# The hidden layer of an MLP by a seven-product form over pairs of chunks, with the output product three pairs behind and interleaved

## The chip, the cores and the metric

One NeuronCore of a Trainium2 chip runs the whole program. The metric is the device time of one launch in microseconds (us), from the first to the last instruction with what lies around it. Two versions count as different here when they differ by more than 0.2%.

## The reference, cut to what matters

Three layers follow one another on 4 x 3072 tokens of width 256: a Fourier mixing layer, a gated layer with hidden width 1024, and an MLP with hidden width 2048. Only the last one is touched:

```
n_tokens, d_model, d_ff = (1536, 256, 2048)     # sizes by which the weights are scaled
...
def _moe2_ref(x, w_in, w_out) -> np.ndarray:
    h = x @ w_in                                  # here x is 12288 x 256, w_in 256 x 2048
    sp = np.where(h > 20.0, h, np.log1p(np.exp(np.minimum(h, 20.0))))
    g = h * np.tanh(sp)                           # Mish
    return (g @ w_out).astype(np.float32)         # w_out 2048 x 256
```

## The kernel before, in words

Every float32 matmul operand is held as two parts, a rounded high part and the remainder (type fp32r), and a product is three matmuls: high by high, high by low, low by high. The table `P3` lists these three.

The MLP is the last stage. The 12288 tokens are cut into 24 tiles (`NBLK`) of 512 columns, and the 2048 hidden features into 16 chunks of 128. A *pair* `P` is two neighbouring chunks of one tile, so a tile has 8 pairs and the stage 192. The input of a tile, `x2`, is 128 partitions by 2 halves of d by 512 tokens; VectorE (DVE) splits it into `x2h` (`split_x2`, line 885). For each pair `emit_h` (line 890) runs `h_mm` twice (line 693 holds the matmul): 2 halves of d times 3 matmuls of 128 x 512 into one PSUM bank. `g_ev` then lets ScalarE (ACT) evaluate Mish twice from PSUM, once rounded into `gh` (line 713) and once in full into `g` (line 714), and DVE subtracts them to `gl` (line 715). `emit_o` (line 898) multiplies `gh` by both parts of `w_out` (one matmul of 512 columns, line 909) and `gl` by the high part (256 columns, line 910), eight such couples per pair, and adds into four PSUM banks `o0` to `o3` that are kept over the tile. At the last pair of a tile `o_out` empties them: an ACT copy (line 923), a DVE add (line 924) and a DMA, for each of the four.

The order is written out by hand: no scheduler moves an instruction, and each engine works through its own queue in the order in which the Python code emits it. The loop over pairs emits h of pair `P`, then the output product of pair `P - LAG`:

```
    LAG = 2
    for P in range(2, 8 * NBLK + LAG):
        ...
            emit_h(P)
            if q == 4 and t + 1 < NBLK:
                split_x2(t + 1)
        emit_o(P - LAG)
```

Pairs 0 and 1 are computed earlier, inside the end of the gated layer. The eight PSUM banks are four for `o` and four for h, which rotate (`bufs=4`).

Of the kernel before, what the change touches and what calls it, by code (L numbers as in the profile page):

```python
# [24 lines left out]
NBLK = B * 6  # L25
# [4 lines left out]
def kernel(  # L30
# [27 lines left out]
    nc = tc.nc  # L58
# [543 lines left out]
    for u in range(NU + 3):  # L602
# [25 lines left out]
        if u in S1_AT:  # L628
            i = 8 + S1_AT[u]
# [28 lines left out]
    def x2h_tile(t):  # L658
        pool = pb if t % 2 else w2p
        x2h_t[t] = pool.tile([128, 2, 2, 512], F32R, tag="x2h", name="x2h", bufs=1)  # L660
        return x2h_t[t]
# [14 lines left out]
    P3 = ((0, 0), (0, 1), (1, 0))  # L676
    g_t = {}
# [9 lines left out]
    def h_mm(f0, p):  # L687
# [3 lines left out]
        for dh in range(2):  # L691
            for (w, v) in P3:
# [3 lines left out]
                )  # L696
                i += 1

    def g_ev(P, ps):

        pool, n = (w2p, 2) if P % 5 < 2 else (pb, 3)
        gh = pool.tile([128, 2, 512], F32R, tag="gh", name="gh", bufs=n)
        gl = pool.tile([128, 2, 512], F32R, tag="gl", name="gl", bufs=n)
# [12 lines left out]
        g_t[P] = (gh, gl)  # L716
# [22 lines left out]
    def emit_k(P):  # L739
        t, i2 = divmod(P, 4)  # L740
        hl = xk_t[t]
        p = psap.tile([128, 2, 512], F32, tag="k", name="kp", bufs=2)
        for m in range(2):
            f = 2 * i2 + m
            i = 0
            for dh in range(2):
                for (w, v) in P3:
                    nc.tensor.matmul(  # L748
                        out=p[:, m, 0:TA], lhsT=WK[:, dh, w, f * 128:(f + 1) * 128], rhs=hl[:, v, dh, :],
                        start=(i == 0), stop=(i == 5),  # L750
                    )
                    i += 1
        kp_t[P] = p
# [43 lines left out]
    def pp():  # L797
        return psap.tile([128, 4, 256], F32, tag="p", name="pp")
# [3 lines left out]
    for t in range(NA + 1):  # L802
        live = t < NA
        nxt = t + 1 < NA
        new = (t + 2) % 8 == 0 and t + 2 < NA
        if new:
            load_Dp((t + 2) // 8)
        for i2 in range(4):
            P = 4 * t + i2
            if live:  # L810
                emit_k(P)
            if 0 <= P - 2 < 4 * NA:
                emit_v(P - 2)
            then = None

            if nxt:
                if i2 == 0:
                    if put:
                        put()
                        put = None  # L820
                    is2_ev(t + 1, 0)
                    is2(t + 1, 1, pp())
                elif i2 == 1:
                    if new:
                        split_Dp((t + 2) // 8)
                    is2_ev(t + 1, 1)
                    delta()
                    if t + 2 < NA:
                        split_D(t + 2)
                elif i2 == 2:  # L830
                    if t > 0:
                        v_ev(t - 1)
                    r_ev(t)
                    if new:
                        prefix((t + 2) // 8, pp()[:, 0:2, :])
                    if t + 2 < NA:
                        split_IF(t + 2)
                    then = shift(t + 1, "xk")
                else:
                    if new:  # L840
                        put = prefix_ev()
                    if t + 2 < NA:
                        is2(t + 2, 0, pp())
                    then = shift(t + 1, "xr")
            elif i2 == 2:
                v_ev(t - 1)
                if live:
                    r_ev(t)
            if i2 == 1 and live:
                emit_r(t)  # L850
            if t == NA - 2 and i2 == 2:
                bg(1 << 20)
                x20 = pap.tile([128, 2, 512], F32, tag="dec_raw", name="x20", bufs=1)
                nc.sync.dma_start(out=x20, in_=x2_part(0, 512))
            if t == NA - 1 and i2 == 0:
                hl = x2h_tile(0)
# [17 lines left out]
    pb = ctx.enter_context(tc.tile_pool(name="pb", bufs=1, side="left", reuse_waits="tile"))  # L874
    psb = ctx.enter_context(tc.tile_pool(name="psb", bufs=1, space=PSUM, reuse_waits="tile"))
    out_v = out.rearrange("(b m w j n) d -> b j m n w d", b=B, m=3, w=32, j=8)

    x2_t, o_t = {}, {}
# [6 lines left out]
    def split_x2(t):
        v = x2_t.pop(t)
        hl = x2h_tile(t)
        split(v, hl[:, 0], hl[:, 1], nc.vector, nc.vector)
# [32 lines left out]
    def o_out(t, m):  # L921
        o, ob = o_t[t][m], ob_t[t]
        nc.scalar.copy(out=ob[:, m, :], in_=o[:, 1, :])
        nc.vector.tensor_tensor(out=ob[:, m, :], in0=ob[:, m, :], in1=o[:, 0, :], op=ALU.add)
        nc.sync.dma_start(out=out_dst(t, m), in_=ob[:, m, :])

    ob_t = {}
    LAG = 2
    load_x2(1)
    load_x2(2)  # L930
    for P in range(2, 8 * NBLK + LAG):
        t, q = divmod(P, 8)
        if P < 8 * NBLK:
            if q == 0 and 2 < t + 2 < NBLK:
                load_x2(t + 2)
            emit_h(P)
            if q == 4 and t + 1 < NBLK:
                split_x2(t + 1)
        emit_o(P - LAG)
# [82 lines left out]
```

## Time and profile before

| what | value |
|---|---|
| median of 3 runs | 2101.23 us (2100.57 to 2104.56) |
| the profiled execution's own time | 2103.25 us |
| its span, first to last instruction | 2101.4 us |
| matmuls (PE) busy | 2051.0 us, 98% of the span |
| weight loads (PEld) busy, beside the matmuls | 1853.3 us, 88% |
| VectorE (DVE) busy | 1108.2 us, 53% |
| ScalarE (ACT) busy | 1069.1 us, 51% |
| GpSimd (POOL) busy | 29.6 us, 1% |

The MLP is roughly the second half of the span, from about 1025 us on. A share of busy time is an average over stages, so what the change is worth has to be read from that half. The recorded length of a matmul (for example 394 ns) covers its way through the array; the next one starts before it ends, so the time that a matmul costs is the distance from its start to the next start, its pitch. In rows that merge several instructions ("x12") the length runs to the start or end of the last.

### The profile page before, as it was taken

The page shows a single profiled execution, that of the slowest core. Times are in us where ns is not written, and L with a number is a line of the kernel's source. Part 1 is how long each engine was busy: PE and PEld are TensorE (multiplying, and loading weights), DVE is VectorE, ACT ScalarE, POOL GpSimd, SP SyncE. Part 2 cuts the span into 40 slices and gives each one's busy share as a digit, 9 for nine tenths or more (in the row PEclk, how much of TensorE's full clock was granted, in tenths as well). Part 3 has the DMA queues.
Part 4 walks back from the last instruction along what each step waited for, and adds up shares of the span by engine and source line. Part 5 has one row for each costly group of instructions (what it writes and reads, how often), then busy time and mean ns, then how long its engine had stood idle before and what let it go on. Part 6 is the DMA issues. An engine that isn't in the chain of part 4 may idle for free.

```text
span 2101.4 us, 28565 instructions
## 1 busy us (share of the span) xinstructions
PE 2051.0 (98%) x11628; PEld 1853.3 (88%) x11628; DVE 1108.2 (53%) x1601; ACT 1069.1 (51%) x1815; POOL 29.6 (1%) x48
## 2 busy tenths in 40 slices
PE   6999998999999999999999999999999999999998
PEld 5999998999999999999988888888888888888887
DVE  5899996787777877776422223222323223223222
ACT  5566655666666666666444434444444344443443
POOL 1000000000000000000000000000000000000000
PEclk6999999999999999999999999999999999999999
DMA  8567532112121121111100000000000000001000
GB/s 249 160 192 209 171 111 74 57 50 73 46 72 51 58 63 56 57 47 44 46 21 21 25 26 21 31 21 21 29 23 30 21 21 21 31 21 31 11 11 20
DMA packets 71476, 122.86 MB, mean 58 GB/s; under 512 B 6193, under 2 KB 48433, under 8 KB 71345
## 3 DMA queue, kind: packets, MB, share of 16 engines
q1 hardware_dynamic: 66864, 105.31, 16.9%
q0 software_dynamic: 4480, 15.73, 2.0%
q8 instruction: 91, 1.49, 0.3%
q14 instruction: 41, 0.33, 0.1%
HBM read 70.69 MB, written 50.33 MB: 58 GB/s over the span
## 4 chain that ended last, share of the span: by engine, by line
PE 79%; DVE 12%; ACT 4%; issue 2%; DMA 2%; SPq 0%; ACTq 0%; DVEq 0%; POOLq 0%
PE hp L693 25%; PE o L909 17%; PE o L910 9%; PE vp L786 8%; PE kp L748 7%; PE mxp L361 5%; PE s2p L315 2%; PE pp L725 2%; PE pp L466 1%; DVE kl L773 1%; PE s1p L274 1%; DVE kr L768 1%; ACT kh L76 1%; PE i1p L385 1%; DVE Dl L77 1%
## 5 line engine op out<-in xcount | busy, mean ns | idle before, releaser
L715 DVE TENSOR_TENSOR gl<-g,gh 128x1024 fp32r<-128x1024 f32 x190 | 232.8, 1225 | 755.1 <-ACT g L714 755.1
L693 PE MATMUL hp<-x2h,WI 128*128 128x512 f32 x2280 | 560.5, 394 | 0.0
L909 PE MATMUL o<-WO,gh 128*128 128x512 f32 x1536 | 546.8, 395 | 0.0
L713 ACT ACTIVATE gh<-hp 128x512 fp32r<-128x512 f32 x380 | 227.2, 598 | 601.8 <-PE hp L693 601.8
L693 PEld LDWEIGHTS hp<-x2h,WI 128*128 128x128 f32 x2280 | 415.2, 188 | 93.0
L910 PE MATMUL o<-WO,gl 128*128 128x256 f32 x1536 | 429.7, 280 | 0.0
L909 PEld LDWEIGHTS o<-WO,gh 128*128 128x128 f32 x1536 | 288.0, 188 | 68.7
L910 PEld LDWEIGHTS o<-WO,gl 128*128 128x128 f32 x1536 | 289.1, 188 | 8.5
L748 PE MATMUL kp<-xk,WK 128*128 128x384 f32 x1536 | 293.0, 339 | 0.0
L786 PE MATMUL vp<-kh,WV 128*128 128x384 f32 x1024 | 283.7, 338 | 6.1 <-DVE r L794 5.9
L748 PEld LDWEIGHTS kp<-xk,WK 128*128 128x128 f32 x1536 | 269.0, 190 | 0.1
L714 ACT ACTIVATE g<-hp 128x512 f32<-128x512 f32 x380 | 225.1, 592 | 0.0
L786 PEld LDWEIGHTS vp<-kh,WV 128*128 128x128 f32 x1024 | 186.3, 188 | 12.7 <-DVE r L794 12.6
L786 PE MATMUL vp<-kl,WV 128*128 128x384 f32 x512 | 171.6, 335 | 0.0
L361 PE MATMUL mxp<-WX,Xh 128*128 128x256 f32 x752 | 140.0, 286 | 0.0
L76 ACT CAST kh<-kr 128x768 fp32r<-128x768 f32 x64 | 53.5, 836 | 153.1 <-DVE kr L768 150.6
L761 ACT ACTIVATE kr<-kp 128x768 f32<-128x768 f32 x128 | 103.9, 812 | 38.5 <-PE kp L748 36.9
L361 PEld LDWEIGHTS mxp<-WX,Xh 128*128 128x128 f32 x752 | 118.5, 194 | 0.2
L361 PE MATMUL mxp<-WX,Xl 128*128 128x256 f32 x376 | 107.1, 285 | 0.0
L773 DVE TENSOR_TENSOR kl<-kr,kh 128x768 fp32r<-128x768 f32 x64 | 62.7, 980 | 69.1 <-ACT kr L772 69.1
L786 PEld LDWEIGHTS vp<-kl,WV 128*128 128x128 f32 x512 | 96.2, 188 | 0.0
L77 DVE TENSOR_TENSOR kl<-kr,kh 128x768 fp32r<-128x768 f32 x64 | 61.4, 959 | 61.4 <-ACT kh L76 61.4
(127 smaller groups left out, 2326.3 us busy)
## 6 DMA issues: line engine op xcount, KB each, us to landing
xs<-in_x_dram SPq DMA_DIRECT2D x32, 384.0 KB
A<-scr SPq DMA_DIRECT2D x48, 256.0 KB
scr<-Cs SPq DMA_DIRECT2D x48, 256.0 KB
D<-scr SPq DMA_DIRECT2D x32, 384.0 KB
x2d<-r POOLq DMA_DIRECT2D x32, 384.0 KB, 3.5
x<-x2d SPq DMA_DIRECT2D x24, 512.0 KB
out_dram<-ob SPq DMA_DIRECT2D x96, 128.0 KB
scr<-st SPq DMA_DIRECT2D x24, 384.0 KB
```

What stands on the lines that cost most here:

```text
L77: (lo_eng or nc.vector).tensor_tensor(out=lo, in0=src, in1=hi, op=ALU.subtract)
L361: nc.tensor.matmul(out=p[:, e, :], lhsT=a, rhs=WX[:, dh, c, w, :], start=(i == 0), stop=(i == 11))
L693: nc.tensor.matmul(out=p, lhsT=WI[:, dh, w, f * 128:(f + 1) * 128], rhs=hl[:, v, dh, :], start=(i == 0), stop=(i == 5),)
L713: nc.scalar.activation(out=gh[:, m, :], in_=p, func=AF.Mish)
L714: nc.scalar.activation(out=g[:, m, :], in_=p, func=AF.Mish)
L715: nc.vector.tensor_tensor(out=gl, in0=g, in1=gh, op=ALU.subtract)
L748: nc.tensor.matmul(out=p[:, m, 0:TA], lhsT=WK[:, dh, w, f * 128:(f + 1) * 128], rhs=hl[:, v, dh, :], start=(i == 0), stop=(i == 5),)
L761: nc.scalar.activation(out=kr, in_=v, func=AF.Relu)
L773: nc.vector.tensor_tensor(out=kl, in0=kr, in1=kh, op=ALU.subtract)
L786: nc.tensor.matmul(out=p[:, o, 0:TA], lhsT=WV[:, f, w, o * 128:(o + 1) * 128], rhs=v[:, m, :], start=(f == 0 and i == 0), stop=(f == 7 and ...
L909: nc.tensor.matmul(out=o[m], lhsT=gh[:, m2, ms], rhs=WO[:, f], start=(f == 0), stop=False)
L910: nc.tensor.matmul(out=o[m][:, 0, :], lhsT=gl[:, m2, ms], rhs=WO[:, f, 0, :], start=False, stop=(f == 15))
```

## The change

Tile 0 keeps the old form. From tile 1 on, a pair of chunks, the two halves of d and the two halves of the tile's 512 columns form 2 x 2 blocks on each side, and h is computed with seven block products in place of eight. A block product (`prod` in `emit_hS`) is three matmuls of 128 x 256, so a pair has 21 of them in place of 12 of 128 x 512. The sums of weight blocks (`WS`, four per pair, high and low part) are made once during tile 0 by `make_WS`; the sums of input blocks (`xS`, seven blocks, high and low part) are made for every tile by `make_xS` in six pieces during the tile before. The products fall into four PSUM banks: `p1` (bank h0), `pA` (h1), `pB` (h2) and `pC` (h3), each with one buffer. ACT copies `p1` to SBUF, and four DVE additions put the quarters together in the SBUF tile `C3`, from which Mish is now read (two activations of 128 x 1024 in place of four of 128 x 512). Mish and the subtraction of pair `P` are emitted inside pair `P + 1`. The output product is the same work, now three pairs behind and cut into eight steps, which stand between the products: 2, 3 and 3.

```
@@ g_ev: buffers @@
+    def g_tiles(P):
+        pool = w2p if P % 4 < 2 else pb
+        return [pool.tile([128, 2, 512], F32R, tag=n, name=n, bufs=2) for n in ("gh", "gl")]
-        pool, n = (w2p, 2) if P % 5 < 2 else (pb, 3)
...
-            g = pb.tile([128, 2, 512], F32, tag="g", name="g", bufs=3)
+            g = pb.tile([128, 2, 512], F32, tag="g", name="g", bufs=2)
@@ new functions; split_x2 and x2h_tile go @@
+    WS = pb.tile([128, 8, 4, 2, 128], F32R, name="WS")
+    def make_WS(q):
+        a = pb.tile([128, 2, 2, 2, 128], F32, tag="C3", name="wa", bufs=2)
+        w = WI[:, :, :, 512 * q:512 * (q + 1)]
+        fl = a.rearrange("p j r i n -> p j (r i n)")
+        nc.vector.tensor_tensor(out=fl, in0=w[:, :, 0, :], in1=w[:, :, 1, :], op=ALU.add)
+        sm = pb.tile([128, 2, 4, 128], F32, tag="C3", name="ws", bufs=2)
+        for k, x0, x1, op in (
...
+        ):
+            nc.vector.tensor_tensor(out=sm[:, :, k, :], in0=x0, in1=x1, op=op)
+        split(sm, WS[:, 2 * q:2 * q + 2, :, 0, :], WS[:, 2 * q:2 * q + 2, :, 1, :])
+    def make_xS(t, k):
...
+        if k == 0:
+            sub(0, b12, b11)
+            sub(2, b22, b12)
+        elif k == 1:
+            sub(1, b22, xT[:, 0, :])
+            sub(3, b21, xT[:, 1, :])
+        elif k == 2:
+            nc.vector.tensor_copy(out=xS[:, 0, 3:7, :], in_=xT)
+        elif k == 3:
+            nc.vector.tensor_tensor(out=xS[:, 1, 3:7, :], in0=xT, in1=xS[:, 0, 3:7, :], op=ALU.subtract)
+        elif k == 4:
+            nc.vector.tensor_copy(out=xS[:, 0, 0, :], in_=b11)
+            nc.vector.tensor_copy(out=xS[:, 0, 1:3, :], in_=b2)
+        else:
+            nc.vector.tensor_tensor(out=xS[:, 1, 0, :], in0=b11, in1=xS[:, 0, 0, :], op=ALU.subtract)
+            nc.vector.tensor_tensor(out=xS[:, 1, 1:3, :], in0=b2, in1=xS[:, 0, 1:3, :], op=ALU.subtract)
...
-            p = psb.tile([128, 512], F32, tag="h", name="hp", bufs=4)
+            p = psb.tile([128, 512], F32, tag=f"h{2 * (P % 2) + m}", name="hp", bufs=1)
...
+    def mish_of(P, c):
...
+        def act():
+            nc.scalar.activation(out=gh, in_=c, func=AF.Mish)
+            nc.scalar.activation(out=g, in_=c, func=AF.Mish)
+        def low():
+            nc.vector.tensor_tensor(out=gl, in0=g, in1=gh, op=ALU.subtract)
+    def emit_hS(P, o):
...
+        before = fin[0] or (lambda: None,) * 2
+        prod(p1, A(0, 0), 0)
+        nc.scalar.copy(out=p1s, in_=p1)
+        before[0]()
+        prod(pA[:, 0, :], A(0, 1), 1)
+        prod(pA[:, 1, :], S_(1), 4)
+        add(c[:, 0:5:4, :], pA, both(p1s))
+        if r > 1 and t + 1 < NBLK:
+            make_xS(t + 1, r - 2)
+        o(2)
+        prod(pB[:, 0, :], S_(0), 3)
+        prod(pB[:, 1, :], S_(2), 5)
+        add(wu, pB, both(c[:, 4, :]))
+        before[1]()
+        o(3)
+        prod(pC[:, 0, :], S_(3), 2)
+        prod(pC[:, 1, :], A(1, 1), 6)
+        add(c[:, 1:3, :], pC, wu)
+        add(c[:, 3, :], pB[:, 0, :], wu[:, 1, :])
+        o(3)
+        fin[0] = mish_of(P, c)
@@ emit_o becomes the generator o_steps, with a yield after each couple of matmuls @@
...
@@ the loop @@
-    LAG = 2
+    LAG = 3
...
+            if t:
+                emit_hS(P, o)
+            else:
+                emit_h(P)
+                if q < 6:
+                    make_WS(q - 2)
+                make_xS(1, q - 2)
...
+        o(9)
```

`before[0]` and `before[1]` are the two Mish activations and the subtraction of the pair before. The new form covers 184 of the 192 pairs (tiles 1 to 23).

**PE, a pair in the steady stage.** Before, h of a pair is one run of twelve matmuls, and the sixteen of the output product follow (the rows start at the end of one pair):

```order
L909 MATMUL o_18454<-WO,gh 128x512
L910 MATMUL o_18454<-WO,gl 128x256
L693 MATMUL hp<-x2h,WI 128x512 x12
L909 MATMUL o_18451<-WO,gh 128x512
L910 MATMUL o_18451<-WO,gl 128x256
```

Now the products are runs of 3 or 6 with output steps between them; here `pC` of one pair, the last three steps, then `p1` and `pA` of the next pair:

```order
L970 MATMUL h_21908<-xS,WS 128x256 x3
L970 MATMUL h_21908<-xS,WI 128x256 x3
L1018 MATMUL o_21757<-WO,gh 128x512
L1019 MATMUL o_21757<-WO,gl 128x256
L1018 MATMUL o_21758<-WO,gh 128x512
L1019 MATMUL o_21758<-WO,gl 128x256
L1018 MATMUL o_21758<-WO,gh 128x512
L1019 MATMUL o_21758<-WO,gl 128x256
L970 MATMUL p_21960<-xS,WI 128x256 x3
L970 MATMUL h_21961<-xS,WI 128x256 x3
L970 MATMUL h_21961<-xS,WS 128x256 x3
```

What moved: the twelve wide h matmuls are gone, 21 narrow ones stand in four places of the pair, and the number of output matmuls is unchanged.

**DVE, the pair in which a tile's outputs are emptied.** Before, one subtraction stands between two tiles' work, and the four `ob` additions come in one piece (waits as the program sets them):

```order
L715 TENSOR_TENSOR gl<-g,gh 128x1024 [waits PE_49,Activation_49] x5
L924 TENSOR_TENSOR ob<-ob,o_11283 128x256 [waits Activation_49]
L924 TENSOR_TENSOR ob<-ob,o_11284 128x256 [waits Activation_49]
L924 TENSOR_TENSOR ob<-ob,o_11285 128x256 [waits Activation_49]
L924 TENSOR_TENSOR ob<-ob,o_11286 128x256 [waits Activation_49]
L715 TENSOR_TENSOR gl<-g,gh 128x1024 [waits DVE_49,Activation_49] x3
```

Now (`C` is the tile `C3`; `h_11311` is `pA`, `h_11312` is `pB`, `h_11313` is `pC`):

```order
L973 TENSOR_TENSOR C_11314<-h_11311,p1s 128x2x256 [waits PE_49,Activation_49]
L913 TENSOR_TENSOR xT<-x_10934 128x256 [waits DMAHW7_49]
L913 TENSOR_TENSOR xT<-x_10934 128x256
L1034 TENSOR_TENSOR ob<-ob,o_11004 128x256 [waits Activation_49]
L973 TENSOR_TENSOR wu<-h_11312,C_11314 128x512 [waits DVE_49,PE_49]
L955 TENSOR_TENSOR gl<-g,gh 128x1024
L1034 TENSOR_TENSOR ob<-ob,o_11005 128x256 [waits Activation_49]
L973 TENSOR_TENSOR C_11314<-h_11313,wu 128x512 [waits DVE_49,PE_49]
L973 TENSOR_TENSOR C_11314<-h_11312,wu 128x256
L1034 TENSOR_TENSOR ob<-ob,o_11006 128x256 [waits Activation_49]
L1034 TENSOR_TENSOR ob<-ob,o_11007 128x256 [waits Activation_49]
```

What moved: the subtraction and the `ob` additions now share the queue with the four additions that empty the product banks.

**DVE, the first pairs of the MLP (tile 0).** Before, the pairs need one subtraction each, and the split of the next tile's input comes once:

```order
L709 TENSOR_TENSOR gl<-g_10891,gh 128x512 [waits Activation_49]
L794 TENSOR_TENSOR r<-r,vp 128x768 [waits DMASW5_49,PE_49]
L715 TENSOR_TENSOR gl<-g,gh 128x1024 [waits Activation_49] x3
L74 CAST x2h<-x_10931 128x1024 [waits DMAHW6_49]
L77 TENSOR_TENSOR x2h<-x_10931,x2h 128x1024 [waits DVE_49]
```

Now, for one pair:

```order
L712 TENSOR_TENSOR gl<-g,gh 128x1024 [waits Activation_49]
L892 TENSOR_TENSOR wa<-WI 128x1024
L898 TENSOR_TENSOR ws<-wa 128x2x128 [waits DVE_49]
L898 TENSOR_TENSOR ws<-ws,wa 128x2x128 [waits DVE_49]
L898 TENSOR_TENSOR ws<-wa 128x2x128
L898 TENSOR_TENSOR ws<-wa,ws 128x2x128 [waits DVE_49]
L77 TENSOR_TENSOR WS<-ws,WS 128x8x128 [waits Activation_49]
L913 TENSOR_TENSOR xT<-x_10932 128x256 [waits DMAHW6_49]
L913 TENSOR_TENSOR xT<-x_10932 128x256
```

What moved: four pairs each get six more DVE operations for `WS`, with a wait for an ACT copy (`WS` high part) among them, and the pieces of `xS`.

## Rows read from the trace of the kernel before

**Rows 1.** Busy time by stretch of the span: PE, PEld, DVE, ACT, POOL; PEclk is the granted clock.
```profile
1040.00:1060.00 20.00, 20.00 (x103) 16.89 (x102) 6.73 (x6) 6.96 (x13) 0.00 (x0) 1.00 0.08 27
1500.00:1600.00 100.00, 100.00 (x502) 84.03 (x501) 27.68 (x31) 41.86 (x80) 0.00 (x0) 1.00 0.07 22
```
**Rows 2.** Chain that ended last, in the MLP: start, length, what.
```profile
1042.12 2.77 PE hp L693 x12
1044.89 0.23 PE o L909
1045.12 0.12 PE o L910
...
1047.69 2.77 PE hp L693 x12
```
**Rows 3.** Timeline of PE in the mixing stage, 128 x 256 matmuls with own weights.
```profile
152.22 0.28 PE L361 MATMUL mxp<-WX,Xl 128*128 128x256 f32 x1
152.22 0.31 PEld L361 LDWEIGHTS mxp<-WX,Xh 128*128 128x128 f32 x2
152.34 0.40 PE L361 MATMUL mxp<-WX,Xh 128*128 128x256 f32 x2
152.46 0.19 PEld L361 LDWEIGHTS mxp<-WX,Xl 128*128 128x128 f32 x1
152.58 0.28 PE L361 MATMUL mxp<-WX,Xl 128*128 128x256 f32 x1
```
**Rows 4.** Groups by line and shape: DVE, then ACT (busy us, mean ns | idle before).
```profile
L715 DVE TENSOR_TENSOR gl<-g,gh 128x1024 fp32r<-128x1024 f32 x190 | 232.8, 1225 | 755.1 <-ACT g L714 755.1
L367 DVE TENSOR_TENSOR yt<-mxp,BB 128x512 f32<-128x512 f32 x48 | 32.8, 684 | 2.6 <-issue 2.4 <-PE mxp L361 0.2
L924 DVE TENSOR_TENSOR ob<-ob,o 128x256 f32<-128x256 f32 x96 | 34.1, 416 | 5.2 <-ACT ob L923 5.2
...
L713 ACT ACTIVATE gh<-hp 128x512 fp32r<-128x512 f32 x380 | 227.2, 598 | 601.8 <-PE hp L693 601.8
L76 ACT CAST xh<-xs 96x1024 fp32r<-96x1024 f32 x32 | 33.6, 1049 | 10.3 <-DMA xs<-in_x_dram 6.9 <-PE s1p L274 3.4
L923 ACT COPY ob<-o 128x256 f32<-128x256 f32 x96 | 36.0, 375 | 22.5 <-PE o L910 21.3
```
**Rows 5.** Timeline in the MLP: handing over from PE to ACT to DVE.
```profile
1500.56 2.92 PE L693 MATMUL hp<-x2h,WI 128*128 128x512 f32 x12
1502.14 0.60 ACT L713 ACTIVATE gh<-hp 128x512 fp32r<-128x512 f32 x1 [3.11 <-PE hp L693]
1502.64 0.59 ACT L714 ACTIVATE g<-hp 128x512 f32<-128x512 f32 x1
...
1504.01 0.59 ACT L714 ACTIVATE g<-hp 128x512 f32<-128x512 f32 x1
...
1504.63 1.22 DVE L715 TENSOR_TENSOR gl<-g,gh 128x1024 fp32r<-128x1024 f32 x1 [4.34 <-ACT g L714]
```
**Rows 6.** Timeline of DVE: operations back to back.
```profile
1040.47 1.22 DVE L715 TENSOR_TENSOR gl<-g,gh 128x1024 fp32r<-128x1024 f32 x1 [4.38 <-ACT g L714]
1041.61 0.68 DVE L74 CAST x2h<-x 128x1024 fp32r<-128x1024 f32 x1
```
**Rows 7.** Start of the MLP: chain row of PE, timeline row of DVE.
```profile
1025.36 2.76 PE hp L693 x12
...
1029.27 1.23 DVE L715 TENSOR_TENSOR gl<-g,gh 128x1024 fp32r<-128x1024 f32 x1 [2.92 <-ACT g L714]
```
**Rows 8.** As rows 1, near the start of the program.
```profile
12.00:16.00 4.00, 1.95 (x15) 1.75 (x14) 2.86 (x4) 3.31 (x6) 0.67 (x1) 0.98 0.95 240
16.00:20.00 4.00, 3.34 (x16) 3.02 (x15) 3.86 (x6) 2.23 (x4) 0.52 (x1) 0.50 0.98 261
...
56.00:60.00 4.00, 4.00 (x21) 4.00 (x20) 1.56 (x2) 2.26 (x3) 0.00 (x0) 0.50 0.01 2
60.00:64.00 4.00, 4.00 (x36) 4.00 (x36) 2.90 (x4) 0.88 (x2) 0.00 (x0) 0.97 0.02 4
```

More of the change, by code (lines that the diff above doesn't have):

```diff
@@ L656 @@
     x2h_t = {}
[L658 to L661, printed above, removed]
     pa = tc.tile_pool(name="pa", bufs=1, side="right", reuse_waits="tile")
@@ L697, in h_mm @@
                 i += 1
+    def g_tiles(P):
+        pool = w2p if P % 4 < 2 else pb
+        return [pool.tile([128, 2, 512], F32R, tag=n, name=n, bufs=2) for n in ("gh", "gl")]
     def g_ev(P, ps):
-        pool, n = (w2p, 2) if P % 5 < 2 else (pb, 3)
-        gh = pool.tile([128, 2, 512], F32R, tag="gh", name="gh", bufs=n)
-        gl = pool.tile([128, 2, 512], F32R, tag="gl", name="gl", bufs=n)
+        gh, gl = g_tiles(P)
         if P < 2:
@@ L855 @@
             if t == NA - 1 and i2 == 0:
-                hl = x2h_tile(0)
+                hl = x2h_t[0] = w2p.tile([128, 2, 2, 512], F32R, tag="x2h", name="x2h", bufs=1)
                 split(x20, hl[:, 0], hl[:, 1], nc.gpsimd, nc.vector)
@@ L883, in load_x2, with sub @@
         x2_t[t] = v
[L885 to L888, printed above, removed]
+    WS = pb.tile([128, 8, 4, 2, 128], F32R, name="WS")
[6 more added lines that the diff above has]
+        for k, x0, x1, op in (
+            (0, a[:, 0, :, 1, :], a[:, 1, :, 1, :], ALU.add), (1, sm[:, :, 0, :], a[:, 0, :, 0, :], ALU.subtract),
+            (2, a[:, 0, :, 0, :], a[:, 0, :, 1, :], ALU.subtract), (3, a[:, 1, :, 0, :], sm[:, :, 1, :], ALU.subtract),
+        ):
+            nc.vector.tensor_tensor(out=sm[:, :, k, :], in0=x0, in1=x1, op=op)
+        split(sm, WS[:, 2 * q:2 * q + 2, :, 0, :], WS[:, 2 * q:2 * q + 2, :, 1, :])
+    xS_t, xT_t = {}, {}
+    def make_xS(t, k):
+        v = x2_t[t]
+        b11, b12, b21, b22 = (v[:, j, 256 * h:256 * h + 256] for j in range(2) for h in range(2))
+        if k == 0:
+            xT_t[0] = pb.tile([128, 4, 256], F32, tag="xT", name="xT", bufs=1)
+            xS_t[t] = pb.tile([128, 2, 7, 256], F32R, tag="xS", name="xS", bufs=2)
+        xT, xS = xT_t[0], xS_t[t]
+        def sub(o, x0, x1):
+            nc.vector.tensor_tensor(out=xT[:, o, :], in0=x0, in1=x1, op=ALU.subtract)
+        b2 = v[:, 1, :].rearrange("p (h n) -> p h n", h=2)
+        if k == 0:
+            sub(0, b12, b11)
[13 more added lines that the diff above has]
+            nc.vector.tensor_tensor(out=xS[:, 1, 1:3, :], in0=b2, in1=xS[:, 0, 1:3, :], op=ALU.subtract)
+            x2_t.pop(t)
     def emit_h(P):
@@ L896, in emit_h @@
         g_ev(P, ps)
-    def emit_o(P):
+    fin = [None]
+    def mish_of(P, c):
+        gh, gl = g_tiles(P)
+        g = pb.tile([128, 2, 512], F32, tag="g", name="g", bufs=2)
+        g_t[P] = (gh, gl)
+        c = c[:, 0:4, :].rearrange("p (m h) n -> p m (h n)", m=2)
+        def act():
[3 more added lines that the diff above has]
+            nc.vector.tensor_tensor(out=gl, in0=g, in1=gh, op=ALU.subtract)
+        return act, low
@@ new lines, in emit_hS, with prod, add, both @@
+    def emit_hS(P, o):
+        t, r = divmod(P, 8)
+        xS = xS_t[t]
+        f = [slice(256 * r + 128 * i, 256 * r + 128 * i + 128) for i in range(2)]
+        p1 = psb.tile([128, 256], F32, tag="h0", name="p1", bufs=1)
+        pA, pB, pC = (psb.tile([128, 2, 256], F32, tag=f"h{k}", name=f"h{k}", bufs=1) for k in (1, 2, 3))
+        A = lambda i, j: (lambda l: WI[:, j, l, f[i]])
+        S_ = lambda k: (lambda l: WS[:, r, k, l, :])
+        def prod(out, a, b):
+            for n, (l, v) in enumerate(P3):
+                nc.tensor.matmul(out=out, lhsT=a(l), rhs=xS[:, v, b, :], start=(n == 0), stop=(n == 2))
+        def add(out, x0, x1):
+            nc.vector.tensor_tensor(out=out, in0=x0, in1=x1, op=ALU.add)
+        def both(v):
+            return v.unsqueeze(1).to_broadcast([128, 2, 256])
+        c = pb.tile([128, 5, 256], F32, tag="C3", name="C3", bufs=2)
+        p1s = pb.tile([128, 256], F32, tag="p1s", name="p1s", bufs=2)
+        wu = pb.tile([128, 2, 256], F32, tag="wu", name="wu", bufs=1)
+        before = fin[0] or (lambda: None,) * 2
[19 more added lines that the diff above has]
+        fin[0] = mish_of(P, c)
@@ L899, in emit_o, with new_o, o_steps @@
+    def new_o(t):
+        o_t[t] = [psb.tile([128, 2, 256], F32, tag=f"o{m}", name=f"o{m}") for m in range(4)]
+        ob_t[t] = pb.tile([128, 4, 256], F32, tag="ob", name="ob", bufs=2)
+    def o_steps(P):
         t, q = divmod(P, 8)
         if q == 0:
-            o_t[t] = [psb.tile([128, 2, 256], F32, tag=f"o{m}", name=f"o{m}") for m in range(4)]
-            ob_t[t] = pb.tile([128, 4, 256], F32, tag="ob", name="ob", bufs=2)
+            new_o(t)
         o = o_t[t]
@@ L905, in emit_o @@
         for m in range(4):
-            ms = slice(m * 128, (m + 1) * 128)
             for m2 in range(2):
                 f = 2 * q + m2
+                ms = slice(m * 128, (m + 1) * 128)
                 nc.tensor.matmul(out=o[m], lhsT=gh[:, m2, ms], rhs=WO[:, f], start=(f == 0), stop=False)
@@ L912, in emit_o @@
                 )
-            if q == 7:
-                o_out(t, m)
+                if q == 7 and m2:
+                    o_out(t, m)
+                yield
     def out_dst(t, m):
@@ L932, with o @@
         t, q = divmod(P, 8)
+        steps = o_steps(P - LAG) if P >= LAG else iter(())
+        def o(n):
+            for _ in range(n):
+                next(steps, None)
         if P < 8 * NBLK:
@@ L935 @@
                 load_x2(t + 2)
[L936 to L939, printed above, removed]
+            if t:
[5 more added lines that the diff above has]
+                make_xS(1, q - 2)
+        elif fin[0]:
+            for step in fin[0]:
+                step()
+            fin[0] = None
+        o(9)
     w2_exit = w2.__exit__
```

## The prediction

> **What bounds the kernel now.** I read the busy time by stretch first. In the MLP, PE is busy for every microsecond, at a granted clock of 1.00, while DVE and ACT are busy for 28 and 42 of 100 us [rows 1]. So this half is paid in PE time alone. The chain of waits says in what coin: h of a pair is one run of 2.77 us, twelve matmuls at a pitch of 0.231 us, and the output product follows until the next run, 1047.69 - 1044.89 = 2.80 us, in couples of 0.23 and 0.12 us [rows 2]. A pair costs 5.57 us. Nothing is waited for, so a change can only gain by issuing less PE time, and it loses wherever it makes PE wait.
>
> **PE work removed and added.** The twelve matmuls of 512 columns go (2.77 us) and 21 of 256 columns come. The nearest row has the very shape: in the mixing stage, 128 x 256 matmuls with weights of their own start at 152.22 and 152.58 with two between, 0.36 us for three, a pitch of 0.120 us [rows 3]. The couples of the output product show the same 0.12 [rows 2]. So h costs 21 x 0.120 = 2.52 us and a pair 2.52 + 2.80 = 5.32 us. Per pair 0.25 us is saved, over 184 pairs **46 us**. The gain is less than the eighth by which the columns shrink (5376 against 6144), since two narrow matmuls cost 0.24 where a wide one cost 0.231.
> The Trainium skill, page "TensorE: Matmul & The Clock Gate", section "Back-to-back issue gap", gives columns / 2.4 + 2.5 ns: 109 and 216 ns, with which h would fall from 2.59 to 2.29 us and the gain be an estimated 55 us. The rows measure 120 and 231 ns, and I go by the rows; the page's rate is a rival below.
>
> **Switching between products.** The run of products is cut in four places by output steps. Before, PE switches from output to h and back once a pair, and the run still measures 2.77 = 12 x 0.231 [rows 2], so a switch with its wait met costs nothing. That is the value I take. The other end: at each switch a weight load stands bare. A load is recorded at 0.19 us [rows 3] against a pitch of 0.12, so 0.07 us, four times a pair: 0.28 us, 52 us over 184 pairs.
>
> **DVE and ACT in a steady pair.** Added to DVE per pair are three additions of 512 and one of 256 from PSUM: 0.684, 0.684, 0.684, 0.416 [rows 4]. None with a broadcast operand or a strided output is in the trace; I price them by their size. With the subtraction (1.225) this is 3.69 us. Per tile come the six pieces of `xS`: four subtractions of 256 (0.416 each), a copy of 1024 (0.68, rows 6 have it), a subtraction of 1024 (1.225), copies of 256 and 512 (some 0.7 together), subtractions of 256 and 512 (1.10): 5.4 us; and the four `ob` additions, 1.66. A tile's sum is 8 x 3.69 + 5.4 + 1.66 = 36.6 us, against 8 x 5.32 = 42.6 us of PE. DVE would be 86% busy: close, but covered.
> ACT per pair: a copy of 256 (0.375), two Mish of 1024. Not in the trace; two of 512 side by side give 2 x 0.598 as the upper end, their pitch of 0.50 doubled gives 0.99 [rows 5], and a copy of 96 x 1024 takes 1.05 [rows 4]. I take 1.05 each, 2.5 us with the copy: covered.
>
> **What PE waits for in a pair.** Count from the first matmul of `p1`: `p1` issues until 0.36, `pA` until 1.08, two output steps (0.35 each) until 1.78, `pB` until 2.50, three steps until 3.55, `pC` until 4.27, three steps until 5.32. A reader sees a product 0.20 us after its last issue (six matmuls from 1500.56 end issue at 1501.94, Mish starts at 1502.14), and ACT hands to DVE within 0.03 (1504.01 + 0.59, then 1504.63) [rows 5]. Each bank has one buffer, and the tight one is `pB`: the next pair's `pB`, at 5.32 + 1.78 = 7.10, must wait for the last addition, which reads `pB` after `pC` is in. DVE in an ordinary pair, with the longest `xS` piece: first addition 1.28 to 1.96, `xS` to 3.1, `wu` to 3.7, subtraction to 4.9, `pC` addition to 5.5, last addition to 5.9. That leaves 1.2 us: **no wait**. The output's `gh` and `gl` are one whole pair early.
> In the pair that empties a tile the queue is longer. The first `ob` addition waits for an ACT copy that stands behind both Mish; these run from 0.93, with a pitch near 0.95, so the copy ends at about 3.2. Then `ob` to 3.6, `wu` to 4.2, subtraction to 5.4, `ob` to 5.7, `pC` addition to 6.4, last addition to 6.7: 0.4 us in time, with the 0.08 us by which neighbours on DVE overlap (1.22 recorded, 1.14 from start to start) [rows 6]. Without that overlap it ends at 7.3 with the handing over and PE stands 0.3 us. I take 0; the other end is 0.35 x 23 tiles = 8 us.
>
> **The first tile is where PE will stand.** Tile 0 still has old pairs, but tile 1 may not start before `xS` is ready, and that stands behind `WS` on DVE. In each of pairs 2 to 5 one DVE turn is: subtraction 1.23, `wa` 1.14, four operations of 256 at about 0.42 = 1.7, a wait for the ACT copy of 1024 (1.05, rows 4), and beside the low part of `WS` and an `xS` piece (2.1) the next pair's four Mish, which sit behind that copy (4 x 0.49 + 0.1 = 2.07), until its subtraction can start. About 7.4 us with the handing over, where the pair itself takes 5.57. The first subtraction is at 1029.27 [rows 7], the fifth (pair 6) therefore at 1058.9. After it come its 1.23, the copies 0.7, the subtraction of pair 7 1.23 and the last piece 1.1: 1063.2. PE has six h runs and five output products ahead of tile 1, from 1025.36 [rows 7]: 1025.36 + 6 x 2.77 + 5 x 2.80 = 1056.0. PE idles from 1056.0 to about 1060.5, when the high parts arrive, and issues only a few matmuls until 1063.2. It is 0.5 us of work ahead, so **6.7 us** are lost. Ends: 4 (operations of 256 at 0.33 and no wait for ACT) and 9.
> Such a hole also takes the clock. Early in the trace PE is busy for 1.95 of 4 us, and the next stretch runs at 0.50, that is 1.2 GHz; the dense stretch from 56 us is still at 0.50 for 4 us, and then at 0.97 [rows 8]. Some 4.5 us at half rate lose 2.3 us; ends 0 and 3.5. Together **9 us** for the start, 4 to 12.
>
> **The end.** Three pairs of output instead of two follow the last h. The Mish of the last pair needs about 4.5 us after it, and two output products (5.6 us) cover that. The total of output matmuls is unchanged. Cost 0; without that cover it would be a single wait of up to 4.5 us.
>
> **Sum.** The profiled execution took 2103.25 us, 2.0 above the median of the runs. 2103.25 - 46 + 9 = 2066.3; against the median, 2101.2 - 46 + 9 = **2064 us**, which I forecast.
>
> **Rivals.**
> - *Small waits*: the tile-emptying pair stalls (8 us) and one switch in four shows 0.05 us (9 us): 2064 + 17 = 2081. For it: 0.4 us of margin rests on an overlap. Against: ordinary pairs have 1.2. Chance 0.17.
> - *PE at the cleaner pitch*: mixed runs could come nearer to plain streaming. The narrowest price that the rows allow is that the output couple, 0.35, has its 0.12 and the wide one 0.231; if a narrow one costs half of that, 0.1155, h is 2.43 us and the gain 63 us: 2047 with the start's 9. Halfway, 2055. The rate of the Trainium skill named above would give 2101 - 55 + 9 = 2055 too. Against: rows 3 hold 0.120. Chance 0.08 around 2055.
> - *Weight loads bare at every switch*: the 52 us above eat the gain: 2101 - 46 + 52 + 9 = 2116, slower. If half of them are bare it is 2090, within 0.2% between. Against: rows 2. Chance 0.05.
> - *DVE becomes the bound*, slower: if the four additions with broadcast or strided operands cost half as much again (2.47 to 3.70 us), DVE needs 5.80 us a pair, more than the 5.57 of before: 2101 + 184 x 0.23 + 9 = 2152. It decides from 5.32 on (a third more on the additions), and turns the sign from 5.57 (40%). Also the loop from last addition over two Mish, subtraction and two additions back to itself (2.1 + 1.23 + 1.1 + 0.2 = 4.6 us) would have to exceed 5.32. Against: the row with PSUM and SBUF operands has 0.684 at 512. Chance 0.05.
> - *No overlap of weight loads with 256 columns*: each matmul lasts a load, 0.19: 21 x 0.19 = 3.99, and 2101 + 184 x 1.22 + 9 = 2334. Rows 3 speak against it: the pitch is 0.12 with loads of 0.19 inside. Chance 0.02. The Trainium skill, same page, section "What overlaps and what doesn't", lets loads overlap running matmuls only in other row groups, which would mean this; the trace disagrees, with full-height loads under running matmuls.
>
> **How the numbers follow.** Forecast 0.63; small waits 0.17; cleaner pitch 0.08: faster by over 0.2% (what a measurement here can tell from none) 0.88. From the bare loads 0.02 falls within 0.2%. Slower: 0.03 + 0.05 + 0.02 = 0.10. The forecast with its bounds (start 4 to 12, pitch 0.120 within 0.002 or 8 us) covers 2051 to 2075; the range reaches up over the small waits and some of the half-bare loads: 2050 to 2090.
>
> **What would show it.** Right: the group of product matmuls with 3864 of them at a pitch of 0.120 and none of 512 columns for h after tile 0; 5.32 us between the starts of `p1`; PE 100% busy in tiles 2 to 23, DVE near 80 to 86%, ACT near 50%; one hole of 5 to 8 us in PE before tile 1, ended by the last `xS` subtractions on DVE, with a granted clock near 0.5 behind it. Wrong: idle time of PE before `pB` in every pair or tile, additions from PSUM above 0.9 us, a pitch of the products above 0.125, or no hole at tile 1.

## The result

The change takes 2052.57 us (median of 4 runs, 2050.61 to 2054.83) against 2102.89 us before: ratio 0.9758, 95% interval 0.9746 to 0.9769. The forecast was 2064 us, range 2050 to 2090. The direction and the range held; the gain is 50 us where 37 were forecast.

The profiled execution took 2050.79 us with a span of 2049.0 us. Its busy times and the groups that are new, from the page of the changed kernel (busy us, mean ns | idle before, and what ended it):

```profile
PE 1994.8 (97%) x13284; PEld 1896.1 (93%) x13284; DVE 1590.5 (78%) x2545; ACT 1094.4 (53%) x1635; POOL 29.6 (1%) x48
...
L970 PE MATMUL h<-xS,WS 128*128 128x256 f32 x2208 | 351.9, 282 | 0.0
...
L973 DVE TENSOR_TENSOR C<-h,p1s 128x512 f32<-128x512 f32 x184 | 127.0, 690 | 163.9 <-PE h L970 163.9
...
L973 DVE TENSOR_TENSOR wu<-h,C 128x512 f32<-128x512 f32 x184 | 126.5, 687 | 37.5 <-PE h L970 33.6
```

DVE's additions cost what their size said (690 and 687 ns, priced at 684 from [rows 4]), also with the broadcast operand and the strided output. DVE is idle before the first addition of a pair, waiting for PE: it has room, and PE has none. Two stretches in the manner of [rows 1], one in the steady stage and one at the start of tile 1 (in order: length, PE, PEld, DVE, ACT, POOL, granted clock, DMA share, GB/s):

```profile
1500.00:1600.00 100.00, 100.00 (x702) 93.39 (x701) 79.62 (x129) 46.24 (x65) 0.00 (x0) 1.00 0.09 26
```
```profile
1054.00:1058.00 4.00, 1.20 (x5) 1.04 (x6) 3.70 (x6) 1.49 (x4) 0.00 (x0) 0.81 0.00 0
1058.00:1064.00 6.00, 6.00 (x28) 5.52 (x27) 1.38 (x2) 0.36 (x1) 0.00 (x0) 0.56 0.27 87
```

In the steady stage PE is busy throughout, as before, now with 80 of 100 us of DVE beside it. The chain of waits shows the pair, to be set beside [rows 2]:

```profile
1504.13 0.36 PE p L970 x3
1504.49 0.71 PE h L970 x6
...
1509.42 0.36 PE p L970 x3
```

From one `p1` to the next are 5.29 us (5.32 forecast), and runs of six products take 0.71 us, 0.118 each (0.1183 from start to start, averaged over the trace from 1100 to 2000 us).

**Where the 50 us came from.** The first half of the program does the same work, yet its length differs from execution to execution: the first h matmul of the MLP starts at 1025.2 us in the profile of before and at 1021.4 in this one (1028.0 in a run below). I therefore compare the MLP by itself, from its first h matmul to the last start of an output matmul, in the two groups of before and the two of after (here and in later fences: min/median/max ns, first and last start):

```profile
L693 PE MATMUL hp<-x2h,WI x2280: 387/394/403, 1025.2 to 2084.8; 128*128 128x512 f32 x190
...
L909 PE MATMUL o<-WO,gh x1536: 388/394/403, 1028.0 to 2093.1; 128*128 128x512 f32 x192
```
```profile
L688 PE MATMUL hp<-x2h,WI x72: 387/390/404, 1021.4 to 1049.0; 128*128 128x512 f32 x72
...
L1018 PE MATMUL o<-WO,gh x1536: 388/394/628, 1026.9 to 2040.7; 128*128 128x512 f32 x192
```

That is 1067.9 us before and 1019.3 after: 48.6 us gained. A pair of before, averaged over the 189 from first to last run, is (2084.8 - 1025.2 - 11 x 0.231) / 189 = 5.593 us; of after, 5.287 us (`p1` of the second new pair at 1065.34 in the chain, the last one at 2027.51, 182 pairs). 184 x 0.306 = 56.3 us gained, and the rest, 7.7 us, is given back where tile 1 starts.

### The profile page after: what moved, and what is told of

The parts are those of the page before. It is cut to its first block, busy times and chain, and to the rows that moved or that the text cites. A ratio compares the mean times of both kernels' runs of the same rounds, so it can differ in the third digit from the quotient of the medians.

```text
span 2049.0 us, 33355 instructions
## 1 busy us (share of the span) xinstructions
PE 1994.8 (97%) x13284; PEld 1896.1 (93%) x13284; DVE 1590.5 (78%) x2545; ACT 1094.4 (53%) x1635; POOL 29.6 (1%) x48
## 4 chain that ended last, share of the span: by engine, by line
PE 76%; DVE 14%; ACT 5%; issue 3%; DMA 2%; SPq 0%; ACTq 0%; DVEq 0%; POOLq 0%
PE h L970 19%; PE o L1018 17%; PE o L1019 9%; PE vp L783 8%; PE kp L745 7%; PE mxp L361 5%; PE p L970 3%; PE s2p L315 2%; PE pp L722 2%; PE pp L466 1%; DVE kl L770 1%; PE s1p L274 1%; DVE kr L765 1%; ACT kh L76 1%; DVE Dl L77 1%
## 5 line engine op out<-in xcount | busy, mean ns | idle before, releaser
L970 PE MATMUL h<-xS,WS 128*128 128x256 f32 x2208 | 351.9, 282 | 0.0
L983 ACT COPY p1s<-p 128x256 f32<-128x256 f32 x184 | 68.5, 372 | 478.5 <-PE p L970 477.5
L970 PEld LDWEIGHTS h<-xS,WS 128*128 128x128 f32 x2208 | 300.6, 189 | 16.1
L973 DVE TENSOR_TENSOR C<-h,p1s 128x512 f32<-128x512 f32 x184 | 127.0, 690 | 163.9 <-PE h L970 163.9
L951 ACT ACTIVATE gh<-C 128x1024 fp32r<-128x1024 f32 x184 | 195.7, 1064 | 10.8 <-DVE C L973 10.8
L952 ACT ACTIVATE g<-C 128x1024 f32<-128x1024 f32 x184 | 193.0, 1049 | 0.0
L970 PE MATMUL h<-xS,WI 128*128 128x256 f32 x1104 | 190.2, 281 | 0.0
L973 DVE TENSOR_TENSOR C<-h,wu 128x512 f32<-128x512 f32 x368 | 187.3, 550 | 1.8 <-PE h L970 1.8
L970 PEld LDWEIGHTS h<-xS,WI 128*128 128x128 f32 x1104 | 156.1, 189 | 0.0
L973 DVE TENSOR_TENSOR wu<-h,C 128x512 f32<-128x512 f32 x184 | 126.5, 687 | 37.5 <-PE h L970 33.6
```

The source lines that it names most:

```text
L951: nc.scalar.activation(out=gh, in_=c, func=AF.Mish)
L952: nc.scalar.activation(out=g, in_=c, func=AF.Mish)
L970: nc.tensor.matmul(out=out, lhsT=a(l), rhs=xS[:, v, b, :], start=(n == 0), stop=(n == 2))
L973: nc.vector.tensor_tensor(out=out, in0=x0, in1=x1, op=ALU.add)
L983: nc.scalar.copy(out=p1s, in_=p1)
```

## The experiments

Each run is set against the kernel before on the same chip, with medians of 2103.66 (first four), 2103.70 (next four) and 2104.56 us (last three). Where a few us matter, the length of the MLP as above stands beside the ratio, since the spread of the first half is not in it. It comes from one profiled execution each; the changed kernel, profiled twice, gave 1019.3 and 1018.4 us.

**The lag alone.** The kernel before with `LAG = 3` and two Mish buffers of each kind:

```
-        pool, n = (w2p, 2) if P % 5 < 2 else (pb, 3)
+        pool, n = (w2p, 2) if P % 4 < 2 else (pb, 2)
...
-    LAG = 2
+    LAG = 3
```

> The kernel before with only the lag of the output product raised from two to three pairs, and the Mish buffers cut as in the change (two of each instead of three). Theory (the whole gain is PE time of the seven products): within 2 us of before, 2101 to 2105, since PE has no idle time in the MLP of before that a longer lag could fill. Rival (the lag or the buffers carry part of the gain or cost something): more than 4 us off, down to 2090 if the lag gave a quarter of the 50 us.

Measured: 2105.79 us, ratio 1.0011 (1.0002 to 1.0021). The lag brings no part of the gain; with the fewer buffers it costs some 2 us, less than the 0.2% that count here.

**Narrow matmuls alone.** The kernel before, each product of h in two halves of 256 columns:

```
+        for s in (slice(0, 256), slice(256, 512)):
...
-                    out=p, lhsT=WI[:, dh, w, f * 128:(f + 1) * 128], rhs=hl[:, v, dh, :],
+                    out=p[:, s], lhsT=WI[:, dh, w, f * 128:(f + 1) * 128], rhs=hl[:, v, dh, s],
```

> The kernel before with each 512-column matmul of h done as two of 256 columns (24 per pair instead of 12, same products, same order of stages). It prices narrow matmuls by themselves. If a narrow one costs 0.1177 us, as the products of the change show, h takes 2.825 us a pair against the 2.79 of before: 192 x 0.03 to 0.055 = 6 to 11 us slower, 2108 to 2114. If it costs the 0.120 of the mixing stage, on which the prediction's sum went: 2.88 us, 192 x 0.09 to 0.11 = 17 to 21 us slower, about 2121. With a bare weight load at each (0.188): 4.5 us, over 300 us slower.

Measured: 2117.17 us, ratio 1.0065 (1.0048 to 1.0082), 13.5 us slower. Its chain of waits shows why it falls between the two ends:

```profile
1503.01 2.86 PE hp L694 x24
1505.87 0.23 PE o L910
```

2.86 / 24 = 0.119 us. So eight products of this size would cost more than the wide form; seven cost less, and the product that is left out is the whole gain. And the price depends a little on the run: from start to start 0.1189 on average in 24 at a stretch, 0.1183 in the change.

**More work on DVE.** The changed kernel with the first addition of each pair done twice, then three times:

```
         add(c[:, 0:5:4, :], pA, both(p1s))
+        add(c[:, 0:5:4, :], pA, both(p1s))
```

> The changed kernel with the first addition of every pair (pA plus the copy of p1) done twice, to the same place: 0.60 us more of DVE per pair, 184 times 0.6 = 110 us of work. Theory (PE is the bound and DVE has about 1.1 us free in an ordinary pair, 0.47 us in the pair that empties a tile): ordinary pairs hide it, PE waits only around the emptying pairs, 0.2 to 0.6 us per tile, so 3 to 14 us slower than the change, 2055 to 2067. Rival (DVE already sets the pace together with PE): 60 us or more slower than the change, above 2110.

> As the run with one more addition, but two more: 1.2 us of DVE more per pair, which brings DVE from 4.21 to about 5.4 us a pair, over the 5.29 of PE. Theory (threshold where DVE's sum passes PE's period): the excess of 0.1 to 0.25 us per pair appears, 20 to 50 us slower than the change, 2073 to 2103, and PE shows waits for DVE before pB in most pairs. Rival (linear from the start): 220 us slower, about 2270. Rival (DVE has more room than the busy share says): below 2065.

Measured: 2055.84 us with one more (ratio 0.9774, 0.9760 to 0.9789), 2107.83 us with two more (1.0021, 1.0011 to 1.0030). The same 100 us of the steady stage, first with one more, then with two:

```profile
1500.00:1600.00 100.00, 100.00 (x702) 93.20 (x701) 91.28 (x149) 47.74 (x67) 0.00 (x0) 1.00 0.09 27
```
```profile
1500.00:1600.00 100.00, 97.31 (x665) 88.86 (x666) 97.38 (x158) 45.62 (x62) 0.00 (x0) 1.00 0.08 23
```

With one more, DVE is at 91%, the profile shows no idle time of PE, and the MLP is as long as without (1023.9 to 2043.3 us). The starts of the matmuls do show a wait of 0.07 us at `pB` once per tile, in the second pair behind the one that empties a tile (0.2 to 0.6 us per tile were expected). In the chain the six products there take 0.78 us in place of 0.71:

```profile
1507.62 0.78 PE h L970 x6
```

That is 1.5 us in all, and in this execution the start of tile 1 was shorter by as much. So of 110 us of DVE work all but 1.5 are hidden. With two more DVE is all but full and PE waits, by the starts of its matmuls in about half the pairs, 0.1 to 0.9 us each; the MLP grows by 52.7 us. This is a threshold, though the run went some us beyond the 20 to 50 that I had expected. The last expectation's figure of 5.4 us per pair took DVE as dense; at 97% with waits for ACT and PE a pair comes to 5.58 us. It marks the edge of the change: DVE has between 0.6 and 1.2 us per pair to spare, and without them the gain is gone.

**The products in one run.** The changed kernel without output steps between the products:

```
-        o(2)
...
-        o(3)
...
-        o(3)
+        o(8)
```

> The changed kernel with the seven products of a pair in one run of 21 matmuls and all eight output steps behind them. Counted from the run's start, pB of the next pair then begins 5.29 + 1.06 = 6.35 us after, 0.7 us earlier against DVE than in the change, while the last addition of an ordinary pair ends near 5.9 (the longest xS piece) or earlier; the pair that empties a tile ends near 6.6 or, with the copies of o behind the outputs, later. Theory (interleaving only buys room for DVE; PE time is a matter of the matmul count): ordinary pairs as before, PE waits only at the emptying pairs, 0.3 to 1.5 us per tile, and if a long run of narrow matmuls costs 0.1192 each as in the run with halves, instead of 0.1178, another 0.03 us a pair: together 10 to 40 us slower than the change, 2062 to 2092. Rival (placing them between the products has no effect at all): within 3 us of the change, 2050 to 2056. Rival (without the placing the form loses its gain): 2095 or more.

Measured: 2061.76 us, ratio 0.9800 (0.9783 to 0.9816); the MLP 1026.3 us, 6.9 to 7.9 longer than in the two profiles of the change. In time it lands just at the low end of what I expected, but not for the reason that I had put first: PE does not wait in the steady stage.

```profile
1500.00:1600.00 100.00, 100.00 (x696) 92.96 (x695) 79.28 (x131) 47.69 (x69) 0.00 (x0) 1.00 0.09 27
```
```profile
1504.74 0.36 PE p L970 x3
1505.11 2.13 PE h L970 x18
```

0.36 + 2.13 to 2.15 us for 21 products is 0.119 each, the price of the long run with halves. By the starts of the matmuls a pair takes 5.330 us, 0.043 more than in the change (8 us over 184 pairs; the start of tile 1 was 1 us shorter in this execution). Only 0.016 of it lies in the products. The larger part, 0.026, lies in the output: in two pairs of every four its second couple takes 0.39 us in place of 0.35.

```profile
1502.25 0.26 PE o L1016
1502.51 0.13 PE o L1017
```

The placing of the output between the products is worth some 7 us through the pitch of PE's matmuls, and, in this schedule, nothing through waits. Why that couple is slow no run tells.

**The hole before tile 1.** PE stands still twice there in the changed kernel, and the chain then shows six products at nearly twice their length until 1063.5 (first fence PE's timeline, second the chain):

```profile
1055.44 0.36 PE L970 MATMUL p<-xS,WI 128*128 128x256 f32 x1 [3.27 <-DVE xS L927]
1057.15 0.79 PE L970 MATMUL p<-xS,WI 128*128 128x256 f32 x2 [1.36 <-DVE xS L930]
```
```profile
1060.51 1.28 PE h L970 x6
...
1063.57 0.71 PE h L970 x6
```

What holds `xS` back is DVE's turn in tile 0, seen in the timelines of DVE and ACT:

```profile
1032.48 1.22 DVE L712 TENSOR_TENSOR gl<-g,gh 128x1024 fp32r<-128x1024 f32 x1
...
1037.55 1.23 DVE L77 TENSOR_TENSOR WS<-ws,WS 128x1024 fp32r<-128x1024 f32 x1 [1.11 <-ACT WS L76]
...
1039.50 1.23 DVE L712 TENSOR_TENSOR gl<-g,gh 128x1024 fp32r<-128x1024 f32 x1
```
```profile
1036.47 1.05 ACT L76 CAST WS<-ws 128x1024 fp32r<-128x1024 f32 x1 [4.01 <-DVE ws L898]
1037.42 0.59 ACT L710 ACTIVATE gh<-hp 128x512 fp32r<-128x512 f32 x1
```

A turn lasts 7.0 us (1032.48 to 1039.50), and the next pair's Mish has to stand behind the ACT copy of `WS`, although its h was ready long before. Behind the wait the granted clock is 0.56 from 1058 to 1064 (shown in the result), so mostly at the lower of its two levels, 1.2 GHz. Three runs go at this. The first has the output two pairs behind (`LAG = 2` in the changed kernel), which gives PE one output product more to do before tile 1:

> The changed kernel with the output two pairs behind instead of three. Theory: in the steady stage nothing changes (the subtraction that the output needs ends over 1 us before it). Before tile 1, PE has one more output product (2.8 us) to do while DVE still makes xS, so the hole of 4.6 us shrinks to some 2 us and, if that is short enough, the granted clock stays at 1.00: 3 to 6 us faster than the change, 2047 to 2050. Rival (the third pair is needed): PE waits for gl in each pair, 0.2 us or more, 2090 or more.

Measured: 2052.57 us, ratio 0.9756 (0.9742 to 0.9771); the MLP 1016.1 us (1027.5 to 2043.6), 2.3 to 3.2 shorter than in the two profiles of the change. The ratio alone does not tell that from nothing; the MLP does. The time stays above the 2047 to 2050 that I expected: the hole shrank, but the clock still fell behind it (last section). No waits for `gl` appear in the steady stage, so the third pair isn't needed there. The second run moves one output product only:

```
             if t:
+                if P == 8:
+                    o(8)
                 emit_hS(P, o)
```

> The changed kernel with the output product of pair 5 moved ahead of tile 1's first product, nothing else. Theory: PE fills 2.8 us of the hole with work that it would do later anyway; the hole shrinks from 4.6 to about 2 us: 2.8 us gained, and up to 2.8 more if the clock then stays at 1.00; 2047 to 2050. Rival (the first pair of tile 1 loses the cover that the output gave to its additions): gained time is given back before pB, within 2 us of the change.

Measured: 2050.47 us, ratio 0.9748 (0.9733 to 0.9762); the MLP 1015.4 us, 3.0 to 3.9 shorter, with the same two waits as with lag two (0.4 and 1.4 us). The third takes the cause away: the copy and the subtraction that make the parts of `WS` come one pair later, behind the next pair's Mish.

```
-        split(sm, WS[:, 2 * q:2 * q + 2, :, 0, :], WS[:, 2 * q:2 * q + 2, :, 1, :])
+        return lambda: split(sm, WS[:, 2 * q:2 * q + 2, :, 0, :], WS[:, 2 * q:2 * q + 2, :, 1, :])
...
                 emit_h(P)
+                if 2 < q < 7:
+                    ws_split()
                 if q < 6:
-                    make_WS(q - 2)
+                    ws_split = make_WS(q - 2)
```

> The changed kernel with the high and low parts of each WS made one pair later in tile 0, behind the next pair's Mish on ACT. It takes away the 7.0 us turn of sums, ACT copy, Mish, subtraction: DVE no longer waits 1.1 us four times, and ACT evaluates Mish as soon as h is there. Theory (the hole before tile 1 is DVE's turn in tile 0, and the half clock behind it follows from the hole): xS is complete near 1053 instead of 1057.7, PE waits under 1.5 us, the granted clock stays at 1.00; 5 to 8 us faster than the change, 2045 to 2048. Rival (something else holds tile 1 back, such as the load of x2 or the banks): under 2 us gained. Rival (the hole goes, but the clock falls all the same): 4 to 5 us gained with 0.50 in a stretch behind 1053.

Measured: 2047.63 us, ratio 0.9733 (0.9719 to 0.9748); the MLP is some 7.5 us shorter. I ran it again beside the changed kernel, with both on one chip:

> The changed kernel itself, as the measure for the two runs beside it on this chip: 2050 to 2055, some 50 us below before.

> The kernel with the parts of WS made one pair later (as measured once), against the changed kernel on the same chip. Theory (the hole before tile 1 and the half clock behind it cost 7.5 us and are gone): 5 to 8 us below the changed kernel. Rival (what was measured was the spread of the first half of the program between executions): within 2 us of it.

Measured: 2054.77 us for the changed kernel (0.9766, 0.9751 to 0.9780) and 2048.52 us for this one (0.9735, 0.9721 to 0.9750), 6.3 us apart; the two intervals do not overlap. The stretch around the start of tile 1, first in the changed kernel, then in this one:

```profile
1045.00:1065.00 20.00, 15.57 (x78) 13.02 (x77) 16.27 (x24) 8.91 (x17) 0.00 (x0) 0.89 0.00 1
```
```profile
1045.00:1065.00 20.00, 20.00 (x116) 17.36 (x115) 16.47 (x25) 7.96 (x14) 0.00 (x0) 1.00 0.09 27
```

No idle time, clock 1.00 (also from 1055 to 1075), and the MLP 1011.8 against 1018.4 us (6.6). The group of output matmuls also loses its longest ones:

```profile
L1018 PE MATMUL o<-WO,gh x1536: 388/394/423, 1033.5 to 2039.8; 128*128 128x512 f32 x192
```

In the change the slowest took 628 ns; here 423. So the hole costs about 4.6 us of waiting and 2 to 3 us of work at half the clock, and both go with their cause. This kernel is faster than the change.

**Output steps one by one.** On top of that version, `o(1)` after `p1` and after each block product but the last, `o(2)` at the end:

> The same kernel with the eight output steps placed singly: one after p1 and after each single block product of pA and pB and the first of pC, two at the end. Runs of narrow matmuls are then 3 long. If a run of narrow matmuls is paced by its weight loads and the first ones behind a wide matmul are cheaper (0.1178 each in runs of 6, 0.119 in runs of 21 to 24), h falls by another 0.01 to 0.03 us a pair: 2 to 5 us faster than the kernel with runs of 6. If not, within 1.5 us of it. Rival (more places where a product has to wait for its bank, or c is ready later for Mish): 2 us or more slower.

Measured: 2074.28 us, ratio 0.9857 (0.9841 to 0.9874), 26 us slower than the version with runs of six: neither of my first two ends. Two things show. In the pair that empties a tile, the `ob` addition is now emitted ahead of the first product addition on DVE (timeline of DVE; then, by what ended it, the idle time of PE's weight loads and of its matmuls):

```profile
1506.66 0.42 DVE L1038 TENSOR_TENSOR ob<-ob,o 128x256 f32<-128x256 f32 x1 [2.38 <-ACT ob L1037]
1507.00 0.68 DVE L973 TENSOR_TENSOR C<-h,p1s 128x512 f32<-128x512 f32 x1
```
```profile
PEld h L970 <- issue: 22.6, 22, 1.1
PE h L970 <- DVE C L973: 16.2, 22, 0.8
```

DVE stands 2.4 us for an ACT copy that is queued behind both Mish, the additions slip, and PE waits for its bank in 22 tiles, up to 0.8 us each in the list of waits. By the starts of `p1` the pair in which it waits, the one behind the emptying pair, takes 6.24 us, 0.95 more than in the change, and that is some 21 of the 26 us. It is the rival "small waits" of the prediction made real by one step out of place. Beyond it, ordinary pairs are not quicker either: half of them take 5.27 to 5.29 us, as in the change, and the other half 5.34. In the chain two runs of three that begin such a pair start at 1520.51 and 1525.85:

```profile
1520.51 0.36 PE p L970 x3
...
1525.46 0.26 PE o L1022
1525.72 0.13 PE o L1023
1525.85 0.36 PE p L970 x3
```

The pitch of the runs is much the same (0.118), and the last couple of such a pair takes 0.39 us in place of 0.35, as one couple does with the products in one run. In both runs it stands in two pairs of every four, those whose `gh` and `gl` lie in the pool `pb` and not in `w2p` (`P % 4` chooses). Whether that is the cause I don't know; no run here tells it. My idea that shorter runs are cheaper did not hold.

## Why the prediction was right, and where it was off

**PE bound before and after: right.** The steady stage has PE at 100 of 100 us in both, the saving is PE time per pair, and the two runs that change only the lag or only the width of the matmuls show no other source.

**The sum's main term was too small.** I put 46 us (5.57 to 5.32 us per pair); measured are 56.3 us (5.593 to 5.287). Both prices were off by a little. The pair of before was read from one period of the chain, 1042.12 to 1047.69; the average over 189 pairs is 0.023 us longer. And the narrow matmul was priced at the mixing stage's 0.120 [rows 3], where the products take 0.1183; with it the pair is 0.033 us shorter. Times 184, these two make the 10.3 us. The run with halves (0.119) shows that the price of a narrow matmul depends on what it runs among. The rival of the cleaner pitch, at 2055 us the nearest to the result, was therefore right in its direction: 0.1183 lies between my 0.120 and its 0.1155. The estimate by the rate that the Trainium skill's page "TensorE: Matmul & The Clock Gate" gives under "Back-to-back issue gap", 55 us, came close to the 56.3, but by luck and not by its parts: the rows have 0.118 and 0.231 us where it has 0.109 and 0.216, and its differences cancel.

**Switching costs nothing: right.** Four switches a pair, and the pair is no longer than its matmuls at their pitch.

**DVE and ACT hide: right, with the margin as worked out.** In the pair that empties a tile I had the last addition ending 0.4 us before `pB` needs its bank. In the trace of the change:

```profile
1498.97 1.01 DVE L973 TENSOR_TENSOR C<-h,wu 128x512 f32<-128x512 f32 x2
...
1500.45 0.76 PE L970 MATMUL h<-xS,WS 128*128 128x256 f32 x5
```

It ends at 1499.98 and `pB` starts at 1500.45: 0.47 us. No idle time of PE is put down to it. DVE's share was forecast at 86% and is 80%, because the sum took each operation at full length (these add up to 87 us in the 100 us shown) and neighbours overlap by 0.08 us [rows 6]. The rival of DVE as the bound is real at two more additions per pair, not before. At that point it costs the whole gain, as the rival's price (from 5.57 us on, slower) had it.

**The hole: right in cause and nearly in size.** Forecast 6.7 us of waiting and 2.3 of half clock, 9 together; measured 7.7, of which 4.6 are waits and some 3 half clock. The turn was put at 7.4 us and is 7.0. That the wait and the slow clock share one cause, and go together, the run with the later split shows; that it was the turn on ACT and DVE, not the data of `x2` or the banks, too.

**Weight loads.** No run shows them bare: the products start 0.118 us apart, each with a recorded load of 0.189 us on a full tile.

```profile
L970 PEld LDWEIGHTS h<-xS,WS 128*128 128x128 f32 x2208 | 300.6, 189 | 16.1
```

The Trainium skill, page "TensorE: Matmul & The Clock Gate", section "What overlaps and what doesn't", lets a load overlap running matmuls only where the row groups differ. The runs disagree with it.

So the error of 13 us in the gain is 10.3 in the main term, 1.3 in the hole, and 1.7 that the MLP doesn't hold, within the spread of the first half.

## What to carry to other kernels

Where PE is busy without a gap, an algorithm with fewer products pays, but count it in measured pitches of the new shape, averaged over many periods and not one, since the narrow shape gives back part of the saving. The work that it puts on other engines is free until their sum per period, or one queue's order, reaches PE's period; here two additions of 0.6 us each per pair were the whole distance between a gain of 2.4% and none. Look for the one-off preparation that stands in a queue with the old work: moving a copy behind what others wait for removed a hole and the slow clock after it.

## What the runs showed of the hardware that I had not expected

A short hole was enough to lose the clock. In the run with lag two, PE waits only 0.41 and 1.36 us, with one matmul between, and the windows around it show (columns as above):

```profile
1061.00:1064.00 3.00, 1.24 (x7) 0.74 (x6) 2.81 (x6) 0.78 (x3) 0.00 (x0) 1.00 0.00 0
1064.00:1067.00 3.00, 3.00 (x13) 2.81 (x14) 0.69 (x1) 0.17 (x1) 0.00 (x0) 0.50 0.51 160
```

After 3 us with PE busy for 1.24, three dense microseconds run at 0.50 (1.2 GHz). In the run with one output product moved, the same two windows have 0.75 and 0.68. This is why the runs that only shortened the hole gained 2 to 4 us and not the 5 to 6 that a kept clock would have given. And a narrow matmul has no single price: 0.118 us in runs of six between wide ones, 0.119 in runs of 21 and 24, 0.120 in the mixing stage.
